# Two sets of sixteen small loads added to the load queue of a decode layer with attention over 32 cached heads and a gated feed-forward

## The chip, the cores and the metric

The kernel runs on one core of one Trainium2 chip. The metric is the device time of one execution in microseconds (us). The kernel before takes 745.52 us, the median of three runs (745.4 to 745.55).

## The reference

One token x (1 x 576) is normalized to xn, and the output is x + attention(xn) + feed-forward(xn), all in float32:

```python
xn = _layernorm(x)
q = (xn @ wq)                                   # 32 heads x 128
scores = einsum("bhqd,bhkd->bhqk", q, k_cache) * (128 ** -0.5)   # 8192 keys a head
o = einsum("bhqk,bhkd->bhqd", softmax(scores), v_cache)
attention = o.reshape(1, 1, 4096) @ wo
gate, up = xn @ W_gate, xn @ W_up               # 576 x 4608 each
feed_forward = ((gate * (gate > 0)) * up) @ W_down
```

The two caches hold 32 heads x 8192 keys x 128 numbers each, 128 MiB each. Nothing of them is used twice: the work is to read some 319 MB once.

## The kernel before, in words

All large inputs are laid out by the host as tiles of 128 rows (partitions) with up to 16384 float32 a row, 64 KiB, so a full tile is 8 MiB. Three buffers (slots 0 to 2) in the on-chip memory take these tiles in turn: first wq, then two tiles of weights for q, gate and up, then 32 tiles of `kv`, one a head, then the tile `vw`, then the output weights `wod`. Tile n of `kv` has in its second half the keys of head n, and in its first half the values of head n-1 (for tile 0 more weights of the feed-forward).

For one head, VectorE multiplies the 128 x 8192 keys by the head's query (L292), sums over the 128 numbers of each key (L297), and takes the largest score of each row (L298, the mark `mr`). TensorE spreads that maximum over the partitions, ScalarE takes the exponentials (L311), and TensorE multiplies them with the values in 64 columns of weights (the mark `V`). The heads go through TensorE three at a time in a loop.

SyncE issues all the large loads (L162) in one queue, in the order of the program: three tiles at once, then each further tile when its slot is free. Its issue waits on the marks of the work that read the slot's last tile: tile n waits for `V` of head n-4 and `mr` of head n-3. What stands behind a waiting load in SyncE's program waits with it. The issue itself does not wait for the transfer: a tile issued while another still moves stands in line behind it. Each load that is issued ends with an increment of a semaphore.

The output weights come last, in chunks: 28 columns of weights into slot 0 (8064 KB), then five chunks of 9, 7, 5, 4 and 3 into slot 1, and then two of 2 and 1 into slot 2 (576 and 288 KB). The chunks of slot 2 wait until TensorE is done with the last values and with the first nine output columns (which came with `vw`). TensorE multiplies chunk by chunk as they land. The sums of all but the last four columns go through VectorE into `x2` (L422, the mark `y`) and are added through TensorE to the last four; VectorE copies the result out (L423, the mark `end`), and SyncE stores it (L185) in four rows of 576 bytes.

```python
    load(("t", 3), 6, kv[3], ("u2", ("mr", 0)), "land2")
    for n in range(4, H):
        load(("t", n), n + 3, kv[n], (("V", n - 4), ("mr", n - 3)), f"land{(n - 1) % G}" if n < H - 1 else "dlast")
```

The change touches `build`: the part that lists SyncE's loads.

Of the kernel before, what the change touches and what calls it, by code (L numbers as in the profile page):

```python
# [9 lines left out]
P = 128  # L10
# [20 lines left out]


STEP = 16

HEAD = 4


class Program:
# [19 lines left out]
    def add(self, engine, f, waits=(), mark=None, on=None, by=1):  # L58
        to = None
        if mark is not None:  # L60
            to = on or engine
            self.sem(to)
            self.counts[to] += by
            assert mark not in self.marks, mark
            self.marks[mark] = (to, self.counts[to])
        self.lists[engine].append((f, tuple(waits), to, by))
# [14 lines left out]
    def emit(self, engine, eng):  # L81
        lines = self.lists[engine]
        if engine == "tensor":
            begin, end, times = self.loop
            self.run(eng, lines[:begin])
            with self.nc.Fori(STEP, STEP * (times + 1), STEP, engines=[PE_ENGINE], head_slot={PE_ENGINE: HEAD}) as i:
                self.run(eng, lines[begin:end], i)
# [20 lines left out]
def build(nc, x, kv, vw, wq, wqt, wg, wod, out):  # L108
    pr = Program(nc)
    add = pr.add  # L110

    def sb(name, shape):
        return nc.alloc_sbuf_tensor(name, list(shape), F32).ap()
# [8 lines left out]
    ones = sb("ones", [P, 1])  # L122
    one = ones[:1, :]
    eps = sb("eps", [1, 1])
    sm = sb("sm", [1, 8])


# [9 lines left out]
    total4 = sb("total4", [P, Q])  # L137
# [22 lines left out]
    def load(name, k, src, waits, on, start=0):  # L160
        dst = slots[k % 3][:, start:start + src.shape[-1]]
        add("sync", lambda e: e.dma_start(dst, src), waits, name, on=on, by=16)  # L162

    def tile(n):
        return slots[(n + 3) % 3]

    load("wq", 0, wq, (), "dwq")
    load("g0", 1, wqt, (), "dg0")
    load("g1", 2, wg, (), "dg1")
# [1 line left out]
    load(("t", 1), 4, kv[1], ("u0",), "land0")  # L171
    load(("t", 2), 5, kv[2], ("u1",), "land1")
    load(("t", 3), 6, kv[3], ("u2", ("mr", 0)), "land2")
    for n in range(4, H):
        load(("t", n), n + 3, kv[n], (("V", n - 4), ("mr", n - 3)), f"land{(n - 1) % G}" if n < H - 1 else "dlast")
    load(("t", H), H + 3, vw, (("V", H - 4), ("mr", H - 3)), "dvw")
    f = OUT[0][0]
    for k, loads in enumerate(OUT[1:]):
        free = ((("V", H - 3), ("mr", H - 2)), (("V", H - 2), ("mr", H - 1)), (("V", H - 1), "u3", ("first", OUT[0][0] - 1)))[k]
        i = 0  # L180
        for n in loads:
            load(("o", f), H + 4 + k, wod[:, (f - 9) * D:(f - 9 + n) * D], free, f"do{f}", i * D)
            i += n
            f += n
    add("sync", lambda e: e.dma_start(out.rearrange("o (j q) -> (o j) q", j=4), total4[0:P:32, :]), ("end",), "out", on="dout", by=16)  # L185


    add("gpsimd", lambda e: e.memset(ident, 0.0), (), "id0")
# [38 lines left out]
    for k in range(36):  # L227
        if k < 32:
            r, a, j = k // 16, k // 4 % 4, k % 4
            mm(("wq", "xz") if k == 0 else (), None, bq[32 * j:32 * j + 32, :], xz[:, a, 5 - r:37 - r],  # L230
               slots[0][:, a * 4096 + (4 * r + j) * 512:][:, :512], k < 4, False)
        else:
            j = k - 32
# [42 lines left out]
    def spread(k, heads):  # L276
        free = ("q", k - 1) if k else ("qs", 1)
        for m, h in enumerate(heads):
            add("scalar", lambda e, m=m, h=h: e.activation(dq[:, m, :], ident, AF.Copy, scale=qs[:, h:h + 1]),  # L279
                (free,) if m == 0 else (), ("dq", k) if m == len(heads) - 1 else None, on="dq" if k else "dq0", by=STEP)  # L280

# [12 lines left out]
    def sums(h, t):  # L294
        k3 = t.rearrange("p (c d) -> p c d", d=DH)
        s = s2[h % 2]
        add("vector", lambda e: e.reduce_sum(s, k3, axis=AX.X), (("mul", h),), ("sum", h))  # L297
        add("vector", lambda e: e.reduce_max(mr, s, axis=AX.X), (("sum", h),), ("mr", h), on=f"mr{(h - 1) % G}" if 0 < h < H - 1 else None, by=STEP if 0 < h < H - 1 else 1)  # L298

# [8 lines left out]
    def soft(h):  # L308
        i, k = h % G, h // G
        waits = (("nb", h),) + (((("V", h - G),) + ((("pl", k - 1),) if i == 0 else ())) if h >= G else ("pz0",))  # L310
        add("scalar", lambda e: e.activation(pz[:, i, :, 4 * G - 4:4 * G], s2[h % 2].rearrange("p (c b) -> p c b", b=4), AF.Exp,  # L311
                                             bias=nb[h % 2], scale=1.0, accum_out=L[:, i:i + 1]), waits, ("exp", h), on=f"exp{i}", by=STEP)

    def rows(k, h):
        add("scalar", lambda e: e.copy(row, bo), (("V", h),) + ((("ot", k - 1),) if k else ("pqt",)), ("oc", k), on="oc", by=STEP)  # L315

# [24 lines left out]
    for n in range(1, H):  # L341
        k, i = (n - 1) // G, (n - 1) % G
# [52 lines left out]
    f, end = 0, H + FC  # L395
# [88 lines left out]
```

## Time and profile before

| What | us |
|---|---|
| median of three runs | 745.52 |
| the profiled execution | 745.8 |
| its span, first to last instruction | 744.4 |
| VectorE busy (share of the span) | 577.1 (78%) |
| TensorE busy | 296.1 (40%) |
| ScalarE busy | 36.1 (5%) |
| GpSimd busy | 2.1 (0%) |
| time of the 16 transfer engines taken by SyncE's loads | 99.3% |

The profile is of one execution. Its span leaves out what lies before the first and after the last instruction; that is 1.4 us here. The core has 16 transfer (DMA) engines that work side by side; a load of 128 rows is cut into packets, one a row where a row has up to 64 KiB, and one more small packet on each engine that it uses carries the increment of the semaphore. The transfer engines' share tells how much of their joint time was taken by packets. Issuing a load costs SyncE some time of its own, which the profile does not count as busy.

### The profile page before, as it was taken

Reading aid. Unit: us, or ns where it says so; the run is one execution under the profiler, and the core shown is the slowest. Engines: PE = TensorE matmul, PEld = TensorE weight load, DVE = VectorE, ACT = ScalarE, POOL = GpSimd, SP = SyncE. Lnnn points to the kernel's source line nnn. Section 1 sums busy time; section 2 is a strip of 40 time slices with the busy share of each in tenths; the row PEclk is TensorE's granted clock in tenths of the full one; section 3 lists DMA queues with packets and bytes.
Section 4 is the critical chain, followed back from the end, with each engine's and each line's share of the span. In section 5 each row is a group of like instructions: output and inputs, shape, how many; then the busy total and the mean of one; then the engine's idle time right before and its main releaser. Section 6 shows DMA issues by size and latency. Waiting matters only on the chain.

```text
span 744.4 us, 4100 instructions
## 1 busy us (share of the span) xinstructions
PE 296.1 (40%) x1772; PEld 86.0 (12%) x1772; DVE 577.1 (78%) x178; ACT 36.1 (5%) x113; POOL 2.1 (0%) x10
## 2 busy tenths in 40 slices
PE   1554413252343343343344334324324324334676
PEld 1111100010010010010010001001001001001122
DVE  2000189989999999999999999999999999999610
ACT  1000001010010010010000000001001000000000
POOL 1000000000000000000000000000000000000000
PEclk9967755656565565666666666666566566566689
DMA  9999999999999999999999999999999999999997
GB/s 395 451 438 408 445 412 441 440 440 416 444 447 405 447 440 412 444 440 433 426 440 444 412 444 440 412 447 440 419 437 440 440 419 441 444 412 438 435 409 320
DMA packets 6360, 319.30 MB, mean 429 GB/s; under 512 B 711, under 2 KB 717, under 8 KB 1102
## 3 DMA queue, kind: packets, MB, share of 16 engines
q1 hardware_dynamic: 6344, 319.17, 99.3%
q8 instruction: 6, 0.10, 0.0%
q14 instruction: 4, 0.03, 0.0%
q10 hardware_dynamic: 6, 0.00, 0.0%
HBM read 319.16 MB, written 0.00 MB: 429 GB/s over the span
## 4 chain that ended last, share of the span: by engine, by line
DMA 53%; DVE 40%; PE 4%; issue 3%; SPq 0%; ACT 0%; DVEq 0%; ACTq 0%
DMA slot<-in_kv 43%; DVE slot L292 20%; DVE s L297 19%; DMA slot<-in_wqt 5%; DMA slot<-in_wod 5%; PE bank L221 4%; DVE mr L298 0%; DVE nb L301 0%; DVE os L305 0%; SPq L162 0%; DVE rl L304 0%; ACT row L315 0%; DVE x L422 0%; ACT pzs L311 0%; DVEq L102 0%
## 5 line engine op out<-in xcount | busy, mean ns | idle before, releaser
L292 DVE TENSOR_TENSOR slot<-slot,bank 128x8192 f32<-128x8192 f32 x32 | 277.9, 8685 | 82.9 <-PE bank L221 52.4
L297 DVE TENSOR_REDUCE s<-slot 128x64 f32<-128x8192 f32 x32 | 277.6, 8675 | 0.0
L221 PE MATMUL bank<-slot,pzs 128*12 128x512 f32 x1024 | 184.3, 886 | 207.0 <-ACT pzs L311 207.0
L221 PEld LDWEIGHTS bank<-slot,pzs 128*12 128x12 f32 x1024 | 35.2, 123 | 333.5 <-issue 333.3
L221 PE MATMUL bank<-slot,xz 128*32 128x512 f32 x208 | 37.6, 754 | 32.2 <-DMA slot<-in_wq 12.6
L221 PE MATMUL bank<-l,ones 128*128 128x3 f32 (+1 forms) x22 | 6.3, 355 | 99.6 <-ACT pzs L311 99.6
L221 PE MATMUL bank<-ident,mr 128*128 128x128 f32 x64 | 16.3, 338 | 73.6 <-DVE mr L298 73.6
L311 ACT ACTIVATE pzs<-s,nb 128x64 f32<-128x64 f32 x32 | 11.1, 348 | 462.6 <-issue 423.3
L242 DVE TENSOR_SCALAR row<-bank 128x512 f32<-128x512 f32 x1 | 0.7, 690 | 33.7 <-PE bank L221 33.7
L422 DVE TENSOR_TENSOR x<-bank,x 128x288 f32<-128x288 f32 x1 | 0.5, 457 | 27.2 <-PE bank L221 27.2
L221 PEld LDWEIGHTS bank<-ident,mr 128*128 128x128 f32 x64 | 9.9, 194 | 96.5 <-DVE mr L298 96.5
L221 PEld LDWEIGHTS bank<-l,ones 128*128 128x128 f32 x22 | 5.3, 300 | 102.4 <-ACT pzs L311 101.6
L279 ACT ACTIVATE dq<-ident,qs 128x128 f32<-128x128 f32 x32 | 10.7, 392 | 129.4 <-PE bank L221 89.5
L221 PEld LDWEIGHTS bank<-slot,xz 128*32 128x32 f32 x208 | 8.6, 134 | 58.5 <-issue 24.1
L221 PE MATMUL bank<-sel,row 128*128 128x3 f32 (+1 forms) x88 | 11.6, 254 | 7.9 <-ACT row L315 7.9
L221 PE MATMUL bank<-slot,os 128*1 128x288 f32 x128 | 10.9, 483 | 5.0 <-DMA slot<-in_wod 5.0
L221 PEld LDWEIGHTS bank<-sel,row 128*128 128x128 f32 x88 | 10.6, 191 | 17.4 <-ACT row L315 17.4
L221 PE MATMUL bank<-slot,hh 128*1 128x288 f32 (+1 forms) x160 | 10.5, 381 | 3.5 <-DMA slot<-in_wod 3.5
L221 PE MATMUL bank<-dq,ones 128*128 128x384 f32 (+1 forms) x24 | 11.1, 549 | 0.0
L221 PE MATMUL bank<-slot,xt 128*32 128x512 f32 x26 | 6.6, 991 | 9.3 <-DMA slot<-in_wqt 9.3
L315 ACT COPY row<-bank 128x512 f32<-128x512 f32 x11 | 6.4, 586 | 73.2 <-PE bank L221 73.2
L301 DVE TENSOR_REDUCE nb<-bank 128x1 f32<-128x128 f32 x32 | 9.0, 283 | 0.7 <-PE bank L221 0.7
(52 smaller groups left out, 53.1 us busy)
## 6 DMA issues: line engine op xcount, KB each, us to landing
slot<-in_wod SPq DMA_DIRECT2D x1, 8064.0 KB, 39.3
slot<-in_vw SPq DMA_DIRECT2D x1, 7968.0 KB, 39.6
slot<-in_wod SPq DMA_DIRECT2D x1, 2592.0 KB, 25.9
slot<-in_wod SPq DMA_DIRECT2D x1, 2016.0 KB, 30.3
slot<-in_wod SPq DMA_DIRECT2D x1, 1440.0 KB, 33.3
slot<-in_wod SPq DMA_DIRECT2D x1, 1152.0 KB, 35.6
slot<-in_wod SPq DMA_DIRECT2D x1, 864.0 KB, 36.9
slot<-in_wod SPq DMA_DIRECT2D x1, 576.0 KB, 25.6
```

The source lines that it names most:

```text
L221: add("tensor", lambda e: e.matmul(o, lhsT, rhs, start=start, stop=stop), waits, mark)
L242: add("vector", lambda e: e.tensor_scalar_mul(row, bq, SCALE), ("pq", "n7"), "qr")
L279: add("scalar", lambda e, m=m, h=h: e.activation(dq[:, m, :], ident, AF.Copy, scale=qs[:, h:h + 1]), (free,) if m == 0 else (), ("dq", k) ...
L292: add("vector", lambda e: e.tensor_mul(k3, k3, qb[:, m, None, :].to_broadcast([P, C, DH])), waits, ("mul", h))
L297: add("vector", lambda e: e.reduce_sum(s, k3, axis=AX.X), (("mul", h),), ("sum", h))
L301: add("vector", lambda e: e.tensor_reduce(nb[h % 2], pm, axis=AX.X, op=ALU.max, negate=True), (("pm", h),), ("nb", h))
L311: add("scalar", lambda e: e.activation(pz[:, i, :, 4 * G - 4:4 * G], s2[h % 2].rearrange("p (c b) -> p c b", b=4), AF.Exp, bias=nb[h % 2], ...
L315: add("scalar", lambda e: e.copy(row, bo), (("V", h),) + ((("ot", k - 1),) if k else ("pqt",)), ("oc", k), on="oc", by=STEP)
L422: add("vector", lambda e: e.tensor_add(x2, acc[:, :N2], x2), ("sums", "x2"), "y")
```

## The change

A new buffer `seen` of 16 partitions x 400 numbers is allocated. A helper `rows16` issues sixteen loads in SyncE's queue without any wait: the first loads 16 rows of 20 numbers (80 bytes a row) from a `kv` tile to `seen`, the next 15 rows of 19, and so on down to one row of 5 numbers (20 bytes). The first set stands behind the load of tile 3, the second behind the chunk of 3 and ahead of the chunks of 2 and 1. All 32 loads count on one new semaphore, `dseen`. Nothing computes with `seen`. The store of the result waits, besides `end`, for the last load of each set.

```diff
+ROWS = tuple(range(16, 0, -1))
...
+    seen = sb("seen", [16, 400])
...
+    def rows16(name, k):
+        for n in ROWS:
+            add("sync", lambda e, n=n: e.dma_start(seen[:n, (k - 3) * 200 + sum(4 + m for m in range(1, n)):][:, :4 + n], kv[k, :n, :4 + n]), (), (name, n), on="dseen", by=16)
...
     load(("t", 3), 6, kv[3], ("u2", ("mr", 0)), "land2")
+    rows16("r0", 3)
     for n in range(4, H):
...
         i = 0
+        if k == 2:
+            rows16("r1", 4)
         for n in loads:
...
-    add("sync", lambda e: e.dma_start(out.rearrange("o (j q) -> (o j) q", j=4), total4[0:P:32, :]), ("end",), "out", on="dout", by=16)
+    add("sync", lambda e: e.dma_start(out.rearrange("o (j q) -> (o j) q", j=4), total4[0:P:32, :]), ("end", ("r0", 1), ("r1", 1)), "out", on="dout", by=16)
```

On SyncE, at the loads of tiles 0 to 5 of `kv` (tile 0 is the first `in_kv` here; the number behind a name is the slot's), there stands before:

```order
L162 DMA slot0<-in_kv 128x16384 [waits s_tensor]
L162 DMA slot1<-in_kv 128x16384 [waits s_tensor]
L162 DMA slot2<-in_kv 128x16384 [waits s_tensor]
L162 DMA slot0<-in_kv 128x16384 [waits s_vector,s_tensor]
L162 DMA slot1<-in_kv 128x16384 [waits s_mr0,s_tensor]
L162 DMA slot2<-in_kv 128x16384 [waits s_mr1,s_tensor]
```

and in the change, from tile 2 to the fourth of the sixteen:

```order
L165 DMA slot2<-in_kv 128x16384 [waits s_tensor]
L165 DMA slot0<-in_kv 128x16384 [waits s_vector,s_tensor]
L172 DMA seen<-in_kv 16x20
L172 DMA seen<-in_kv 15x19
L172 DMA seen<-in_kv 14x18
L172 DMA seen<-in_kv 13x17
```

Tile 4, which stood right behind tile 3, now stands behind sixteen loads that wait for nothing.

On SyncE, at the program's end, there stands before:

```order
L162 DMA slot1<-in_wod 128x2304 [waits s_vector,s_tensor]
L162 DMA slot1<-in_wod 128x1728 [waits s_vector,s_tensor]
L162 DMA slot2<-in_wod 128x1152 [waits s_tensor]
L162 DMA slot2<-in_wod 128x576 [waits s_tensor]
L185 DMA out_y<-total4 4x144 [waits s_vector]
```

and in the change, from the fourteenth of the second sixteen on:

```order
L172 DMA seen<-in_kv 3x7
L172 DMA seen<-in_kv 2x6
L172 DMA seen<-in_kv 1x5
L165 DMA slot2<-in_wod 128x1152 [waits s_tensor]
L165 DMA slot2<-in_wod 128x576 [waits s_tensor]
L195 DMA out_y<-total4 4x144 [waits s_dseen,s_vector]
```

The last two chunks now stand behind the sixteen, and the store has a second semaphore to wait for.

## Rows read from the trace of the kernel before

**Rows 1.** The page, parts 2 and 3: the transfer engines over the span, and the queues.

```profile
DMA  9999999999999999999999999999999999999997
DMA packets 6360, 319.30 MB, mean 429 GB/s; under 512 B 711, under 2 KB 717, under 8 KB 1102
...
q1 hardware_dynamic: 6344, 319.17, 99.3%
q8 instruction: 6, 0.10, 0.0%
...
q10 hardware_dynamic: 6, 0.00, 0.0%
```

**Rows 2.** Transfers from 500 to 700 us: queue (packets, MB, share), loads (us to landing).

```profile
q1 hardware_dynamic: 1497, 86.59, 100.1%
...
slot<-in_kv SPq DMA_DIRECT2D x8, 40.2
```

**Rows 3.** Transfers from 733 to 738 us, where the packets are small.

```profile
DMA packets 296, 2.06 MB, mean 411 GB/s; under 512 B 33, under 2 KB 33, under 8 KB 173
...
q1 hardware_dynamic: 296, 2.06, 99.2%
```

**Rows 4.** Stretches of 0.5 us at the end: stretch, engines' busy times, clock, DMA share, GB/s.

```profile
739.50:740.00 0.50, 0.17 (x4) 0.10 (x8) 0.00 (x0) 0.00 (x0) 0.00 (x0) 1.00 0.62 244
740.00:740.50 0.50, 0.50 (x16) 0.21 (x8) 0.00 (x0) 0.00 (x0) 0.00 (x0) 1.00 0.41 161
740.50:741.00 0.50, 0.25 (x8) 0.00 (x0) 0.43 (x1) 0.00 (x0) 0.00 (x0) 1.00 0.34 134
741.00:741.50 0.50, 0.42 (x16) 0.36 (x20) 0.03 (x1) 0.00 (x0) 0.00 (x0) 1.00 0.07 28
```

**Rows 5.** Timeline from 739.5 us: start, us, instructions, idle before and what ended it.

```profile
739.84 0.91 PE L221 MATMUL bank<-slot,hh 128*1 128x288 f32 x16 [0.97 <-DMA slot<-in_wod]
740.57 0.46 DVE L422 TENSOR_TENSOR x<-bank,x 128x288 f32<-128x288 f32 x1 [27.20 <-PE bank L221]
741.90 0.11 PEld L221 LDWEIGHTS bank<-slot,hh 128*1 128x1 f32 x8 [0.23 <-DMA slot<-in_wod]
742.40 0.31 DVE L423 COPY total<-bank 128x144 f32<-128x144 f32 x1 [1.38 <-PE bank L221]
742.74 0.65 SPq L185 DMA_DIRECT2D out_y<-total  x1
```

**Rows 6.** Timeline of SyncE, 108 to 130 us: issues of tiles 3 and 4.

```profile
108.52 0.33 SPq L162 DMA_DIRECT2D slot<-in_kv  x1
128.77 0.33 SPq L162 DMA_DIRECT2D slot<-in_kv  x1
```

**Rows 7.** Transfers from 100 to 112 us: the load of tile 3, us to landing.

```profile
slot<-in_kv SPq DMA_DIRECT2D x1, 31.9
```

**Rows 8.** Timeline of SyncE at the end: issues of the chunks (several in a row).

```profile
701.08 0.38 SPq L162 DMA_DIRECT2D slot<-in_wod  x1
701.59 0.34 SPq L162 DMA_DIRECT2D slot<-in_wod  x1
702.04 1.19 SPq L162 DMA_DIRECT2D slot<-in_wod  x2
715.54 0.80 SPq L162 DMA_DIRECT2D slot<-in_wod  x2
```

**Rows 9.** The page, part 6: three chunks, KB each, us from issue to landing.

```profile
slot<-in_wod SPq DMA_DIRECT2D x1, 864.0 KB, 36.9
slot<-in_wod SPq DMA_DIRECT2D x1, 576.0 KB, 25.6
slot<-in_wod SPq DMA_DIRECT2D x1, 288.0 KB, 25.9
```

**Rows 10.** SyncE's waits, 700 us to the end: total, times, longest.

```profile
SPq L162 <- PE bank L221: 12.5, 2, 12.3
SPq L432 <- SPq L432: 1.0, 1, 1.0
```

**Rows 11.** Issue of the load of x, one row, from ScalarE's queue: ns.

```profile
L197 ACTq DMA_DIRECT2D row<-in_x x1: 531/531/531, 0.7 to 0.7; - x1
```

## The prediction
> **What bounds the kernel now.** I read the page's second and third parts first. The transfer engines show a 9 in every slice but the last, and SyncE's queue alone takes 99.3% of the joint time of the 16 engines [rows 1]. So the kernel is bound by reading 319 MB, from the first tile to the last chunk. The chain of waits passes through VectorE too, since its maxima free the slots, but that does not make VectorE a bound: from 500 to 700 us the transfer engines are taken to 100.1% (packets that cross the window's edge), and a tile lands 40.2 us after its issue [rows 2]. At the rate of that window, 86.59 MB in 16 x 200 x 1.001 = 3203 engine-us, or 27.0 bytes a ns on each engine, a tile of 128 packets of 64 KiB takes 8 x 65536 / 27.0 = 19.4 us. So each issue has another tile still in transfer and one's own time behind it: an issue that came 10 us later would cost nothing.
>
> Then I read the end. The share of the engines falls in steps, 0.62, 0.41, 0.34, 0.07, from 739.5 to 741.5 us [rows 4]: the 16 engines do not finish together, the first are done nearly 2 us ahead of the last, and only about one engine in fourteen is busy in the last of these stretches. The last weight loads wait 0.23 us for the last chunk, to 741.90, and 0.5 us later the copy of the result begins [rows 5]. So **the last engine sets the end**, and work that is added to another engine has up to 2 us of room.
>
> **The change, term by term.** It removes nothing. It adds 32 loads to SyncE's program and to the transfer queue, and one wait.
>
> *Packets.* A load of n rows brings n packets of data and a semaphore packet on each engine that it uses. The two loads on queue 10 have one and two rows and left 6 packets [rows 1]: one data and one semaphore packet a row. SyncE's queue agrees: 44 loads of 128 + 16 packets, and the store with 4 + 4, make the 6344. So a set has 2 x (16 + 15 + ... + 1) = 272 packets, both 544, and queue 1 should show 6888.
>
> *Price of a packet.* No row shows loads of 20 to 80 bytes one behind the other. The nearest is the stretch from 733 to 738 us, with 296 packets of mostly 5 to 9 KB, 33 of them under 512 bytes [rows 3]. They took 0.992 x 16 x 5 = 79.4 engine-us; 2.06 MB at 27.0 bytes a ns are 76.3; the rest, 3.1 us over 296 packets, is 10.5 ns a packet. A small load then costs an engine 10.5 + 10.5 + at most 80 / 27 = 3, some 24 ns. Both ends: nothing, if the engine takes them while it waits for other bytes; and 1.0 us, the time from the end of the store's issue to its landing (L432) [rows 10], if each had to be finished before the next begins. I take 24 ns, since semaphore packets between data are already in the 733 to 738 stretch and the share there is still 99.2%.
>
> *Which engine.* If the rows go to engines by their number, the first engine gets 16 loads of a set and the sixteenth gets one. That is 32 x 24 = 0.77 us on the fullest over both sets, 2 x 24 = 0.05 us on the emptiest, and 17 x 24 = 0.41 us on the mean engine. The rows do not say which of them is the one that ends last; I take the mean, 0.41 us, and keep 0 and 0.77 for the range.
> The Trainium skill has a rule here, in "DMA: Bandwidth & Descriptors", section "Why a DMA increments its semaphore by 16 and not by 1": a load from SyncE's queue uses the lowest-numbered engines, as many as divide the slowest dimension. By it the fullest engine gets the 0.77 us; were the rows dealt out evenly, every engine would get 0.41. The packets on queue 10 agree with the count of engines, and no row shows their numbers.
>
> *SyncE's time, first set.* Tile 3 is issued at 108.52 us and tile 4 at 128.77 [rows 6], and between them SyncE waits. A full load's issue takes 0.33 to 0.38 us, at a pitch of 0.45 to 0.51 [rows 8]; those with few rows took more, 0.65 for the store of four rows [rows 5] and 0.53 for the load of one [rows 11]. At the dearer price with a pitch gap, 0.65 + 0.1, sixteen take 12 us, and 19.9 are free. Cost: nothing. If that cover were gone, tile 4 would have 108.52 + 31.9 = 140.4 us, the landing of tile 3 [rows 6, 7], as its date, 11.6 us behind its present issue.
>
> *SyncE's time, second set.* The five chunks are issued by 702.04 + 1.19 = 703.23 us, and the next two at 715.54 after a wait of 12.3 [rows 8, 10]. Sixteen at 0.75 take 12.0 us, so the cover may just hold. If it does not, the chunk of 3 lands only at 702.9 + 36.9 = 739.8 us (its issue is the later half of the row at 702.04) [rows 8, 9], so the chunks of 2 and 1 have 24 us in hand. Cost: nothing.
>
> *The store's second wait.* All small loads stand ahead of the last two chunks on their engines, so `dseen` is full before `end`. Today 0.03 us pass from the copy's end, 742.40 + 0.31 = 742.71, to the store at 742.74 [rows 5]; one more wait that is satisfied already I put at 0.05 us, between nothing and twice that.
>
> *The sum.* 0.41 + 0.05 = 0.46 us. On the profiled execution, 745.8 us, this makes 746.3. That execution lies 0.3 us above the median of the three runs, so the forecast for the median is 745.52 + 0.46 = **746.0 us**, with 745.5 and 746.4 by the ends of the packets' term. Differences under 0.2%, 1.5 us, count as no change.
>
> **Rivals.**
>
> *Slower: the small loads are paid one after the other on the first engine.* Each semaphore packet would hold the engine until its data have landed. For it: the only tiny transfer whose whole way is seen, the store, takes 1.0 us beyond its issue [rows 10]. Against it: the 33 semaphore packets of the 733 to 738 stretch leave no room for such holds [rows 3]; but there 8 data packets stand between two of them on an engine, and here one tiny one. At 1.0 us each, 32 loads put 32 us on the first engine; less its room of 0 to 2 us, 775.5 to 777.5 us. It decides from about 50 ns a load, if the first engine is also the last to end (32 x 0.05 = 1.6 us), and from 110 ns if it is the earliest (3.5 us less 2). At 0.1 us a load it would be 747 to 748.7 us. Chance 0.13.
> The Trainium skill speaks for this: the same page, section "Anatomy of one DMA — SWDGE (gpsimd) path", puts a fixed cost of about 2.0 us on every transfer, which by that page lies mostly in the receipt of the last byte. In sequence, 32 of them would be 64 us, an estimate from that page, and some 810 us. That section is on the other way of issue, and no row here shows its figure: the store's 1.0 us is the whole way seen.
>
> *Slower: the cover of the issues runs out.* It needs 16 issues to take more than 19.9 + 11.6 us in the first set, some 2 us each, or 12.3 + 24 = 36 in the second, 2.3 each; rows 5, 8 and 11 show 0.33 to 0.65. At 2.5 us, 40 - 31.5 = 8.5 us are lost in the first set and 4 in the second: about 758 us. Chance 0.02.
>
> *The small loads do not fall as their rows say*, but evenly on all engines, or as packets that cost nothing. 745.5 to 746.0 us, no change. Chance 0.06.
>
> *Faster.* Nothing is taken away; but the engines that end last also carried the program's code, six packets of 16 KB on queue 8 [rows 1], each 16384 / 27.0 = 0.6 us. Shifted times could put one on another engine: 744.9 us, still no change. Chance 0.04, and half of that for more than one, or another shift, beyond 1.5 us.
>
> **How the numbers follow.** The forecast has 0.75, as no change; with the even spread, 0.06, and the code's half, 0.02, "same" has 0.83. Slower has 0.13 + 0.02 = 0.15, faster 0.02. The range goes from 745.2 us, no cost and a part of a code packet saved, to 747.2, where the packets' price is doubled on the fullest engine (32 x 48 ns = 1.5 us, and 0.05): it holds the forecast with both ends and the cheap foot of the first rival.
>
> **What would show it.** Queue 1 has 6888 packets. SyncE's timeline has sixteen issues from 109 us, each under 0.75 us, ended before tile 4 goes out near 128.8, and sixteen from 703, with the two chunks still near 715.5. Tile 4 onward is issued at the old times to within 0.5 us. The steps of the engines' share at the end keep their form and lie 0.4 us later. I am wrong if the load of tile 4 takes over 1 us more from issue to landing than before, if the last chunks land over 1.5 us later, or if a wait of the store on the new semaphore shows.

## The result, and the profile after

The changed kernel takes 748.9 us, the median of four runs (748.64 to 749.22), against 745.51 us before: a ratio of 1.0046, 95% interval 1.0028 to 1.0063. It is slower by 3.4 us. The forecast was 746.0 us and no change, with a range to 747.2; the time lies above it, and the case that came nearest is the first of the slower rivals (small loads paid one after the other on an engine), at a chance of 0.13. The profiled execution took 748.64 us, its span 747.3, so between the two profiles 2.9 us are to be found.

The count of packets is what the prediction said; the second and third parts of the page show it, beside [rows 1]:

```profile
DMA packets 6904, 319.32 MB, mean 427 GB/s; under 512 B 1255, under 2 KB 1261, under 8 KB 1646
...
q1 hardware_dynamic: 6888, 319.18, 99.2%
```

The share of the transfer engines' time is 99.2%, against 99.3 before, although the bytes are the same and the span is longer. So most of the added time is counted as time in which packets were under way: packets became slower. The transfers from 500 to 700 us tell where that was not so: 86.73 MB moved there, against 86.59 in [rows 2].

```profile
DMA packets 1498, 86.76 MB, mean 434 GB/s; under 512 B 168, under 2 KB 168, under 8 KB 168
...
q1 hardware_dynamic: 1495, 86.73, 100.2%
```

The loss lies at the two sets. From 137 to 143 us, where the first set passes, the kernel before and then the change show:

```profile
DMA packets 51, 2.29 MB, mean 382 GB/s; under 512 B 16, under 2 KB 16, under 8 KB 16
...
q1 hardware_dynamic: 51, 2.29, 88.3%
```

```profile
DMA packets 319, 2.04 MB, mean 340 GB/s; under 512 B 288, under 2 KB 288, under 8 KB 288
...
q1 hardware_dynamic: 319, 2.04, 97.8%
```

288 of the 319 packets are under 512 bytes: the set's 272, and tile 3's 16 increments. In so short a stretch the rates tell little, since whole 64 KiB packets fall in or out at its edges; the lengths of the packets tell more. The small packets themselves are short, 9 ns for an increment and 9 to 12 ns for data in the trace. What grew are the 64 KiB packets behind them: 2418 ns is usual, and the first one behind the set took from 2.6 to 4.6 us, the longest on the engine with 16 small loads. The trace does not name the engines, but on each of them the packets follow without a gap here, so that some can be followed through the set: the first 64 KiB packet took 0.46 us more than usual behind seven small loads, 1.28 behind ten, 1.46 behind eleven and 2.19 behind sixteen.

The end, by the timeline, against [rows 5]:

```profile
741.70 0.46 DVE L432 TENSOR_TENSOR x<-bank,x 128x288 f32<-128x288 f32 x1 [25.93 <-PE bank L231]
742.21 0.43 PE L231 MATMUL bank<-x,pick 128*1 128x144 f32 x8 [0.33 <-DVE x L432]
744.06 0.35 PEld L231 LDWEIGHTS bank<-slot,hh 128*1 128x1 f32 x16 [1.75 <-DMA slot<-in_wod]
744.77 0.10 PEld L231 LDWEIGHTS bank<-slot,hh 128*1 128x1 f32 x8 [0.36 <-DMA slot<-in_wod]
745.26 0.31 DVE L433 COPY total<-bank 128x144 f32<-128x144 f32 x1 [3.11 <-PE bank L231]
745.60 0.62 SPq L195 DMA_DIRECT2D out_y<-total  x1
```

VectorE's sum into `x2` hangs on the chunk of 3, which stands ahead of the second set on the engines. It starts at 741.70 us, 1.13 later than before: what the first set left behind. Then TensorE's weight load waits 1.75 us for the chunk of 2, a wait that was not there before; the second set stands between those two chunks. The copy starts 745.26 - 742.40 = 2.86 us later, so some 1.1 us are the first set's and 1.7 the second's.

SyncE's issues, by its timeline at the two places ([rows 6, 8] are those of before):

```profile
108.69 0.33 SPq L165 DMA_DIRECT2D slot<-in_kv  x1
109.06 6.01 SPq L172 DMA_DIRECT2D seen<-in_kv  x16
135.94 0.36 SPq L165 DMA_DIRECT2D slot<-in_kv  x1
```

```profile
701.78 2.23 SPq L165 DMA_DIRECT2D slot<-in_wod  x5
704.06 19.65 SPq L172 DMA_DIRECT2D seen<-in_kv  x16
723.75 4.74 SPq L165 DMA_DIRECT2D slot<-in_wod  x2
```

The first set is issued in 6.01 us. The second takes 19.65, and the last two chunks go out at 723.75 instead of 715.54 us. The chain of waits of the same kernel, from 700 us on, leads through these issues:

```profile
707.35 0.29 SPq L172
707.65 0.04 issue
707.69 3.66 SPq L172
711.35 0.04 issue
711.39 4.72 SPq L172
...
723.75 20.26 DMA slot<-in_wod
```

Nine issues take 0.3 to 0.4 us, and then single ones take up to 4.72. By this chain SyncE is on the path. Whether these issues cost the time is what has to be tested first.

### The profile page after: what moved, and what is told of

Read it like the earlier page. It is cut to its first block, busy times and chain, and to the rows that moved or that the text cites. A ratio compares the mean times of both kernels' runs of the same rounds, so it can differ in the third digit from the quotient of the medians.

```text
span 747.3 us, 4133 instructions
## 1 busy us (share of the span) xinstructions
PE 293.3 (39%) x1772; PEld 86.6 (12%) x1772; DVE 576.7 (77%) x178; ACT 36.1 (5%) x113; POOL 2.1 (0%) x10
## 3 DMA queue, kind: packets, MB, share of 16 engines
q1 hardware_dynamic: 6888, 319.18, 99.2%
## 4 chain that ended last, share of the span: by engine, by line
DVE 49%; DMA 40%; PE 4%; issue 4%; SPq 3%; ACT 0%; DVEq 0%; ACTq 0%
DMA slot<-in_kv 32%; DVE slot L302 24%; DVE s L307 23%; DMA slot<-in_wqt 5%; PE bank L231 4%; DMA slot<-in_wod 3%; SPq L172 3%; DVE mr L308 1%; DVE nb L311 1%; SPq L165 0%; DVE os L315 0%; DVE rl L314 0%; ACT row L325 0%; DVEq L104 0%; ACT pzs L321 0%
## 5 line engine op out<-in xcount | busy, mean ns | idle before, releaser
L231 PE MATMUL bank<-slot,pzs 128*12 128x512 f32 x1024 | 178.5, 861 | 202.2 <-ACT pzs L321 202.2
L231 PE MATMUL bank<-ident,mr 128*128 128x128 f32 x64 | 18.9, 384 | 79.3 <-DVE mr L308 79.3
L321 ACT ACTIVATE pzs<-s,nb 128x64 f32<-128x64 f32 x32 | 11.1, 348 | 457.0 <-issue 418.3
L231 PEld LDWEIGHTS bank<-ident,mr 128*128 128x128 f32 x64 | 11.6, 227 | 100.5 <-DVE mr L308 100.5
```

Of the source, the lines that this page charges most:

```text
L231: add("tensor", lambda e: e.matmul(o, lhsT, rhs, start=start, stop=stop), waits, mark)
```

## The experiments

Theory A: each transfer engine pays for its own small loads, one after the other, and the engine that ends last sets the end. Rival B: the held-up issues of the second set cost the time. Others came up on the way. In what follows, "lost engine time" is worked out from the semaphore increments in the trace: the mean of the 16 increments of tile 5, less that of tile 3, less two tiles' time of 19.355 us each (undisturbed tiles land 19.35 to 19.36 us apart), times 16. It is -0.1 us in the kernel before and 16.5 us in the changed one.

**The first set alone.**

```diff
-        if k == 2:
-            rows16("r1", 4)
```

> Only the first set stays, behind tile 3. Theory A (each engine pays its own small loads one after the other, about 0.13 us each beyond the first few, and the engine that ends last sets the end): the last landing of tile 5 and of all later tiles comes about 1.0 to 1.4 us later than in the kernel before, and the time is 746.2 to 747.0 us. Rival B (the loss is made at the end, where SyncE's second set of issues took 19.65 us and put the last two chunks' issue off from 715.5 to 723.8 us): 745.5 to 745.8 us here.

Measured: 747.12 us, ratio 1.0023 (1.0013 to 1.0034), 1.5 us more than the 745.63 of before beside it; lost engine time 15.0 us. That is a little above what A gave, and far above B's 745.8. One part of A's expectation fell: the last increment of tile 5 comes only 0.2 us later than in the kernel before, and that of tile 30 1.3 us later. The engine that ends last here was not the last one when the set passed. The end of the timeline has no new wait, only the old order later:

```profile
742.40 0.42 PE L229 MATMUL bank<-x,pick 128*1 128x144 f32 x8 [0.34 <-DVE x L430]
...
743.25 0.10 PEld L229 LDWEIGHTS bank<-slot,hh 128*1 128x1 f32 x8 [0.26 <-DMA slot<-in_wod]
743.75 0.31 DVE L431 COPY total<-bank 128x144 f32<-128x144 f32 x1 [1.41 <-PE bank L229]
```

The copy starts 1.35 us later than in [rows 5]. A set 600 us ahead of the end still costs the end that much: the queues are never empty after it, so an engine that falls behind stays behind. In this trace the 64 KiB packets behind the set show only 6.8 of the 15.0 us; 6.2 more are engine time without any packet under way, which the change's trace does not have.

**The second set alone.**

```diff
-    rows16("r0", 3)
```

> Only the second set stays, ahead of the last two chunks. Theory A: the last engine ends 1.3 to 2.0 us later, 746.8 to 747.6 us; the two parts together make the 3.4 us of the change. Rival B (late issue of the last two chunks): all of it is here, 748.5 to 749.2 us. In both the issues of the set take some 19 us again.

Measured: 747.52 us, ratio 1.0020 (1.0010 to 1.0029), 1.9 us more than before. With the 1.5 us of the first set that makes the 3.4 of the change. By B all of it should have been here. The wait between the chunks of 3 and 2 is back:

```profile
740.78 0.43 PE L230 MATMUL bank<-x,pick 128*1 128x144 f32 x8 [0.33 <-DVE x L431]
742.63 1.06 PEld L230 LDWEIGHTS bank<-slot,hh 128*1 128x1 f32 x24 [1.75 <-DMA slot<-in_wod]
...
744.32 0.31 DVE L432 COPY total<-bank 128x144 f32<-128x144 f32 x1 [3.60 <-PE bank L230]
```

**The second set, but ahead of the five chunks.** Here less is queued on the engines when SyncE issues the set.

```diff
-    rows16("r0", 3)
...
-        if k == 2:
+        if k == 1:
```

> Only the second set, but ahead of the five chunks instead of behind them, so that less is queued on the engines when SyncE issues it. Theory G: the same loss as with the second set behind them, 746.8 to 747.7 us, though its sixteen issues take 6 to 7 us instead of 18 to 20. Rival B (the held-up issues cost something): 745.6 to 746.2 us.

Measured: 747.25 us, ratio 1.0017 (1.0008 to 1.0027), 1.7 us more than the 745.53 beside it. SyncE's timeline:

```profile
681.26 6.22 SPq L172 DMA_DIRECT2D seen<-in_kv  x16
700.45 17.18 SPq L165 DMA_DIRECT2D slot<-in_wod  x7
```

The sixteen issues take 6.22 us and the wait for the freed slot still covers them, and the loss is the same. So the long issues are not what costs the time, and B falls, although the chain of waits runs through them: the two chunks had, as the prediction worked out, 24 us in hand, and were issued 8 us late.

**The same loads, spread.** Two small loads stand behind each of sixteen tiles instead of sixteen in a row at two places.

```diff
-    rows16("r0", 3)
     for n in range(4, H):
         load(("t", n), n + 3, kv[n], ...)
+        if n < 20:
+            rows1("r0", 3, 20 - n)
+            rows1("r1", 4, 20 - n)
...
-        if k == 2:
-            rows16("r1", 4)
```

Here `rows1(name, k, n)` issues the one load of n rows that stood in `rows16`.

> The same 32 small loads, but two behind each of the tiles 4 to 19 instead of sixteen in a row. Theory A in its form with a threshold (an engine works ahead, so a few small loads in a row are hidden and only the further ones cost): each engine pays 12 + 12 ns a load at most, 0.8 us on the fullest, 745.5 to 746.4 us. Rival C (each small load has its price wherever it stands, 0.12 us and more): the fullest engine loses 32 x 0.12 = 3.8 us, 747.5 to 749.5 us.

Measured: 746.28 us, ratio 1.0010 (1.0000 to 1.0020). That is 0.65 us over the 745.63 beside it, inside the range of the theory with a threshold; rival C, that a small load has its price of 0.12 us and more anywhere, falls. The packets and the loads are those of the change. What is dear is their standing in a row.

**One row each.** All 32 loads have one row, at the same two places.

```diff
-... e.dma_start(seen[:n, ...][:, :4 + n], kv[k, :n, :4 + n])
+... e.dma_start(seen[:1, ...][:, :4 + n], kv[k, :1, :4 + n])
```

> All 32 small loads have one row, so that there are 32 data packets instead of 272, all on one engine. Theory A (paid by the engine itself): that engine loses some 2.2 + 1.5 us as the fullest one did; less its room of up to 2 us, 746.5 to 749 us, with one engine's packets stretched and the other fifteen as in the kernel before. Rival D (the small packets disturb what the engines share, in proportion to their number): 1/8 of the loss, 745.6 to 746.0 us.

Measured: 748.67 us, ratio 1.0042 (1.0026 to 1.0059), nearly the change's loss with 32 data packets in place of 272. The lost engine time at the first set is 2.8 us, most of it on one engine. Behind the first set one 64 KiB packet took 4.33 us and the other engines' at most 2.66. Rival D, a loss in proportion to the packets, would have given 746.0 at most and falls. The end shows the one engine at work:

```profile
741.18 0.43 PE L231 MATMUL bank<-x,pick 128*1 128x144 f32 x8 [0.33 <-DVE x L432]
743.52 1.06 PEld L231 LDWEIGHTS bank<-slot,hh 128*1 128x1 f32 x24 [2.24 <-DMA slot<-in_wod]
...
745.21 0.31 DVE L433 COPY total<-bank 128x144 f32<-128x144 f32 x1 [4.08 <-PE bank L231]
```

The chunk of 3 is late by only 0.1 us (the matmuls after it start at 741.18, against 741.08 in the kernel before, below): by this the first set went into that engine's room.

```profile
741.08 0.42 PE L221 MATMUL bank<-x,pick 128*1 128x144 f32 x8 [0.33 <-DVE x L422]
```

After the second set all wait 2.24 us for the chunk of 2. The trace of this run also gives the price: the increments of the sixteen loads of a set arrive 181 to 192 ns apart in the first set and 181 to 197 in the second, while the packets' own records stand 12 to 14 ns apart in the first.

**One load in place of sixteen.** Each set is one load of 16 rows x 16 pieces of 48 bytes: as many data packets on each engine as on the fullest one in the change, and one increment instead of sixteen.

```diff
-        for n in ROWS:
-            ...
+        add("sync", lambda e: e.dma_start(seen[:, (k - 3) * 200:][:, :192].rearrange("p (a b) -> p a b", b=12), kv[k, :16, :].rearrange("p (a b) -> p a b", b=1024)[:, :, :12]), (), (name, 1), on="dseen", by=16)
```

> Each set is one load of 16 rows x 16 pieces of 48 bytes: 16 tiny data packets on every engine as on the fullest one in the change, but one semaphore packet instead of sixteen. Theory G (an engine's semaphore increments are made one after the other, 0.18 us each, as the landings 181 ns apart of the run with one-row loads suggest, and a row of them holds the engine up): 745.6 to 746.3 us. Rival E (each tiny data packet holds the engine, by its read or its write): every engine loses some 16 x 0.13 us a set, 749 to 750.5 us.

Measured: 746.47 us, ratio 1.0014 (1.0005 to 1.0024), 0.8 us more than the 745.68 beside it: 0.2 above what G gave, and far below the 749 of rival E. From 137 to 143 us it has as many small packets as the change, and five 64 KiB packets more:

```profile
DMA packets 324, 2.37 MB, mean 395 GB/s; under 512 B 288, under 2 KB 288, under 8 KB 288
...
q1 hardware_dynamic: 324, 2.37, 95.0%
```

The longest 64 KiB packet behind the set took 2.64 us, and the lost engine time is 4.9 us, 0.3 for each engine. So tiny packets of data are nearly free; what is dear comes once a load on each engine.

**All loads with 16 rows.**

```diff
-... e.dma_start(seen[:n, ...][:, :4 + n], kv[k, :n, :4 + n])
+... e.dma_start(seen[:16, ...][:, :4 + n], kv[k, :16, :4 + n])
```

> All 32 small loads have 16 rows, so that all engines carry what the fullest did: 512 data packets instead of 272. Theory A with G (what counts is the load on the engine that ends last, which had 13 loads a set in the change's trace and has 16 now): 3 x 0.18 us a set more than the change, 749.5 to 750.5 us. Rival D (a loss in proportion to all small packets): 3.4 x 512 / 272 = 6.4 us, 751.5 to 752.5 us.

Measured: 750.69 us, ratio 1.0065 (1.0048 to 1.0082): 5.0 us over the 745.68 beside it, 0.2 above the range of A with G, and 0.8 below that of D. The lost engine time at the first set is 36.1 us, 2.3 for each engine. Against the run with one load, which has the same 512 data packets in all, the sets differ by 240 increments (256 less 16) and 36.1 - 4.9 = 31.2 engine-us: 0.13 us for each increment.

**Six loads of 16 rows in each set.**

```diff
-ROWS = tuple(range(16, 0, -1))
+ROWS = tuple(range(6, 0, -1))
...
+... e.dma_start(seen[:16, ...][:, :4 + n], kv[k, :16, :4 + n])
```

> Each set is six loads of 16 rows instead of sixteen of 16 to 1 rows, so every engine has six in a row. In the change's second set the engines with up to seven small loads lost under 0.15 us, those with more some 0.15 us for each further one. Theory G with that threshold: 745.6 to 746.6 us. Rival H (each load has its 0.18 us from the first on): 12 x 0.18 = 2.2 us on every engine, 747.3 to 748.0 us.

Measured: 746.6 us, ratio 1.0012 (1.0002 to 1.0022), 0.9 us over before: at the upper edge of G with a threshold, below H. The lost engine time is 5.5 us, 0.34 for each engine. From six loads to sixteen an engine loses 2.26 - 0.34 = 1.9 us more, 0.19 for each further load; the first six cost at most 0.06 each. At most, because tile 4 was issued late here, at 136.11 us, and on time in the run with 16 rows, at 128.56: the run with the second set alone, which also issued it late, lost 2.1 us at this place without any small load. Without these 2.1 us the six loads would have cost 0.035 each and a further one 0.20.

**Rows of 512 bytes, first set alone.**

```diff
-    seen = sb("seen", [16, 400])
+    seen = sb("seen", [P, 256])
...
-... e.dma_start(seen[:n, ...][:, :4 + n], kv[k, :n, :4 + n])
+... e.dma_start(seen[16 * (n % 8):16 * (n % 8) + n, n // 9 * 128:][:, :128], kv[k, :n, :128])
...
-        if k == 2:
-            rows16("r1", 4)
```

> Only the first set, with rows of 512 bytes instead of 20 to 80. Theory G: a load's data takes 19 ns longer on an engine, hidden under its 0.18 us: as the run with the first set alone, 746.9 to 747.5 us. Rival F (it is the rows under 512 bytes that are dear): the loss goes, 745.6 to 746.1 us.

Measured: 747.27 us, ratio 1.0021 (1.0011 to 1.0030); lost engine time 17.5 us, where rows of 20 to 80 bytes lost 15.0 and 16.5. Six to twenty-five times the bytes cost the same, so rival F falls.

**A semaphore for each load.**

```diff
-..., (name, n), on="dseen", by=16)
+..., (name, n), on=f"d{name}{n}", by=16)
...
-..., ("end", ("r0", 1), ("r1", 1)), "out", on="dout", by=16)
+..., ("end",) + tuple((r, n) for r in ("r0", "r1") for n in ROWS), "out", on="dout", by=16)
```

> The change with a semaphore of its own for each of the 32 small loads. Theory G (the engine makes its increments one after the other, whatever counter they go to): 748.4 to 749.4 us, as the change. Rival I (increments of one shared counter get in each other's way, between engines or between loads): the loss goes or shrinks, 745.6 to 747.5 us. The store's 31 more waits add up to 1 us by either, seen as a gap between the copy and the store.

Measured: 749.1 us, ratio 1.0043 (1.0026 to 1.0059), lost engine time 16.2 us. The loss is that of the change, so it does not lie in the shared counter, and I falls. The copy ends at 745.97 us and the store goes out at 746.00, so the 31 waits more cost nothing there.

**32 one-row loads in one row, first set alone.**

```diff
-ROWS = tuple(range(16, 0, -1))
+ROWS = tuple(range(32, 0, -1))
...
-    seen = sb("seen", [16, 400])
+    seen = sb("seen", [1, 512])
...
-... e.dma_start(seen[:n, ...][:, :4 + n], kv[k, :n, :4 + n])
+... e.dma_start(seen[:1, 16 * (n - 1):][:, :12], kv[k, :1, :12])
...
-        if k == 2:
-            rows16("r1", 4)
```

> One set of 32 one-row loads in a row behind tile 3, all on one engine, none at the end. In the run with one-row loads 16 in a row took 2.8 engine-us, with six loads of 16 rows an engine lost 0.34. Theory G with a few hidden at first and about 0.2 us for each further load: 5.5 to 6.5 engine-us on one engine, the other fifteen unmoved, and less that engine's room a time of 748.5 to 751 us. If the loss were once for a set (a pause of the engine), 2.8 engine-us and 746 to 747.5 us.

Measured: 748.65 us, ratio 1.0042 (1.0028 to 1.0056). A pause once for a set would have given 747.5 at most. The 32 increments arrive 180 to 192 ns apart here, 5.7 us from first to last, and one 64 KiB packet took 6.6 us. From the increment of tile 3 on, the engine with the small loads lost 5.0 us, a little under the 5.5 to 6.5 expected; in the run with one-row loads the engine with sixteen lost 2.1 us, so a further load costs 0.18 us, the distance between two increments. The expectation that the other fifteen engines stay unmoved did not hold: 11.1 us of engine time were lost in all, several of their packets took 2.6 to 3.0 us, and one 3.8. In this run tile 4 was issued at 135.90 us, 1.8 us before the first engine came to it. The run with the second set alone issued it at 136.0 and lost 2.1 us there without any small load, so I put at least a part of it down to the late issue; how much was not separated.

## Why the prediction was wrong, point by point

**What bounds the kernel** held. The bytes are the same, the middle of the span moves at the same rate, and the last engine sets the end: 32 one-row loads on one engine cost nearly as much (3.0 us) as the change's 272 data packets over all engines (3.4).

**The packets** held: 6888 on queue 1, and in the trace sixteen packets of 80 bytes, fifteen of 76 and so on to one of 20, as if row by row on engines of their own. The rule of the Trainium skill that the prediction weighed ("DMA: Bandwidth & Descriptors", section "Why a DMA increments its semaphore by 16 and not by 1") agrees in the count of the engines: one for each row. That they are the lowest-numbered no row shows.

**The price of a packet is the step that failed**: "A small load then costs an engine 10.5 + 10.5 + at most 80 / 27 = 3, some 24 ns". Increments that follow each other on an engine come 181 to 192 ns apart, and beyond the first six a load costs 0.19 us, eight times the 24 ns. The row that I took the price from [rows 3] had semaphore packets, but between two of them on an engine stood eight data packets of 5 to 9 KB, well over a microsecond of work. A time of 0.18 us for each was not to be seen there: the whole remainder of 3.1 us is 0.09 us for each of the 33 small packets. The rival's paragraph named that very difference and the threshold of 50 ns; I gave it 0.13. Its upper end, 1.0 us a load, was too high, its foot of "0.1 us a load", 747 to 748.7 us, just short of the measured 748.9. The rule that spoke for this rival in the Trainium skill ("DMA: Bandwidth & Descriptors", section "Anatomy of one DMA — SWDGE (gpsimd) path") puts a fixed 2.0 us on a transfer. No run here shows that paid in a row: loads in a row ended 181 to 192 ns apart. The same section calls the time of the semaphore's own write tiny, about one cycle. No run here shows that write by itself; what stands in the 181 ns between two increments stays open.

**Which engine**: I took the mean engine, 17 loads over both sets, and the fullest for the bound. In the changed kernel's trace the engines that came last to the first set had 11, 10 and 7 of its loads, and the one that came last to the second had 13. An engine with n loads loses, as an estimate from the runs with six and sixteen, 0.34 + (n - 6) x 0.19 us: 1.3 us for 11 and 1.7 for 13. The two sets alone cost 1.5 and 1.9 us. By the same estimate the mean engine, 8.5 loads a set, loses 0.8 us a set, 1.6 of the 3.4. So the price was the larger miss, and the choice of the mean engine a second one. The upper end of the range, by its own terms 745.52 + 1.54 + 0.05 = 747.1 us rather than 747.2, fell with the price.

Which engines end last can be read from the increments of the kernel before: at the second tile of weights for q, gate and up, complete at 62.3 us, one of the 16 stands 1.2 us behind the others, at tile 1 two do and at tile 3 three, after code packets of 16 KB (queue 8 of [rows 1]) at 48, 87 and 114 us. By these times the room of up to 2 us comes from the code, at some 1.2 us a packet, where the prediction put 0.6.

**SyncE's time**: the first set was hidden as said. Sixteen issues took 6.01 us, not the 12 that I allowed. For the second set I allowed 12 and saw 19.65; the cover broke as the prediction feared, and the second cover, 24 us until the chunk of 3 lands, held. The run with the set ahead of the five chunks, with its issues covered, loses as much.

**Tile 4's issue** was forecast within 0.5 us of 128.8 and came at 135.94. That is not the set's doing: with the first set alone it went out at 129.35, and with the second alone at 136.0. The page of the change shows 6.9 us of TensorE's waits marked "issue" at the queries of the heads, and that of the kernel before none; why they came in some runs stays open. With the second set alone 2.1 us of engine time were lost at that place, 0.13 for each engine, so as much of the change's 16.5 may be the late issue and not the set.

**The store's wait** cost nothing: the copy ends at 745.57 and the store goes out at 745.60, the 0.03 us of before, where I had put 0.05.

**What would show it** named a later landing of the last chunks by over 1.5 us as the sign of the rival, and this is what came: the last weight loads start 2.87 us later, 744.77 against the 741.90 of [rows 5].

## What to carry to other kernels

In a kernel that the transfer engines bound, a tiny load is priced by how many loads stand in a row on an engine, not by its bytes or packets: here the first six cost at most 0.06 us each and further ones 0.18 to 0.20, on the same engine, and spreading them or making one load of them gave most of it back (746.28 and 746.47 us for 748.9). Where the engines do not end together, price the work on the engine that ends last, and remember that in a queue that is never empty a delay near the start is still there at the end. And a chain that runs through an instruction does not make it the cause: ask what slack the next step has, and move the instruction to see.

## What the runs showed that I had not expected

- Increments of one engine in a row come 180 to 197 ns apart, read where one engine was at work (the runs with one-row loads). The loss is the same with one shared counter and with 32 of their own (16.5 and 16.2 us). That it is the increment, and not something else that comes once a load on an engine, such as a wait until the load's data have landed, was not separated: a load without an increment was not tried.
- SyncE's issue can be held up by what is queued: 6.0 us for sixteen issues behind tile 3, 6.2 behind the chunk of 28, 19.7 with five chunks more ahead of them. In the changed kernel nine issues took under 0.45 us each and then one took 3.66. The chunks need not be there: of the 32 one-row loads behind tile 3, the last two were held as well. What limit that is was not measured.

```profile
118.66 2.36 SPq L172 DMA_DIRECT2D seen<-in_kv  x1
121.07 4.80 SPq L172 DMA_DIRECT2D seen<-in_kv  x1
```

- The time that a 64 KiB packet is held counts as busy: the share was 99.2% with the loss and 99.3% without. The lengths of the packets and the landings of the increments told it. In the runs that issued tile 4 on time (the first set alone, 16 rows, one load) a part of the loss showed as engines without a packet instead: 6.2, 3.1 and 1.8 us of engine time.
